# Strassen-type stage of a top-k attention and two-MoE kernel: parity of deferred cosines, earlier due times of joins and snapshots, one pair fewer on shared banks

## The chip, the core and the metric

The kernel runs on one core of one Trainium2 chip. The metric is the device time of one execution in microseconds (us). Three executions of the kernel before took 1436.85, 1238.50 and 1239.03 us, median 1239.03. The profiled execution took 1239.47 us; the profile's own span, from the first to the last instruction, is 1237.7 us, so 1.8 us lie around it.

## What is computed

```python
def _attn_ref(q, k, v):                 # 4 x 8 heads, 576 tokens, head size 64
    scores = scale * np.matmul(q, k.transpose(0, 1, 3, 2))
    kth = np.partition(scores, -top_k, axis=-1)[..., -top_k:-top_k + 1]   # top_k = 32
    scores = np.where(scores >= kth, scores, -1000000000.0)
    attn = np.exp(scores - np.max(scores, axis=-1, keepdims=True))
    attn = attn / (np.sum(attn, axis=-1, keepdims=True) + 1e-09)
    return np.matmul(attn, v)

def _moe_ref(x, w_gate, w_val, w_out):  # 2304 tokens, 512 -> 1536 -> 512
    g = x @ w_gate
    silu = g * (1.0 / (1.0 + np.exp(-g)))
    return silu * (x @ w_val) @ w_out

def _moe2_ref(x, w_in, w_out):          # 2304 tokens, 512 -> 2048 -> 512
    h = x @ w_in
    return (h * np.cos(h)) @ w_out
```

The three run one after the other on the same 2304 tokens; only the last result is an output.

## The kernel before, in words

Attention and the first MoE run interleaved until about 855 us of the span. The change touches what follows: the second MoE.

**Input stage of the second MoE** (`h_proc`, `row_proc`). `h = x @ w_in` is built for blocks of 576 tokens (4 blocks) and, in each block, for 8 pairs of feature tiles of 128 rows, 32 pairs in all. Pair k of the kernel makes the tiles f = 2i (its row 0) and f = 2i + 1 (its row 1), where i = k mod 8. Each pair is a Strassen-Winograd scheme: seven products of six matmuls of 288 columns (line 1401), into three PSUM banks. Between the products stand three snapshots, copies of a bank to SBUF on ScalarE (two of them line 1432, one line 1488), and four joins on VectorE that add a bank and a snapshot into a piece of a row of h (lines 1445, 1466 and 1473) or copy a bank (line 1479). The seventh product, into the first bank, may start only after the join of line 1466 has read that bank; the last join, line 1479, frees it. The products of the next pair may start once the third product of this one is issued.

The scheme's operands are made on the way: weight combinations (adds on VectorE at line 1268, then a rounded part on ScalarE at line 1284 and the remainder on VectorE at line 1287; seven for each two pairs), and combinations of x (line 1351, line 1368 on ScalarE, line 1372 on VectorE; seven for a block). In names such as `w_14_11544` the first number counts these weight tiles: 0 to 6 belong to pairs 0 and 1 of a block, 7 to 13 to pairs 2 and 3, 14 to 20 to pairs 4 and 5, 21 to 27 to pairs 6 and 7.

**Cosines** (`cosine`). h * cos(h) takes three ScalarE operations (lines 1535, 1548, 1551) and two on VectorE (lines 1543, 1552). Half of the feature tiles get it here, 576 tokens wide, before they are stored to the DRAM tensor `gd`. The other half is stored raw, and gets it in the output stage, 512 elements wide. Which half is said by group number: tiles of groups 1 and 3 (`LATE`) are the deferred ones.

**Output stage** (`piece_proc`, `o_proc`, `wout2_proc`). For each of 18 tiles of 128 tokens and each of the four groups, one DMA brings four feature tiles of `gd` (`gr`), the deferred groups get their cosine, the piece is split into a rounded part and a remainder (lines 1643 and 1647), and 12 matmuls of 512 columns (line 1672) add it to the output bank with the weight tiles `W2O` (lines 1589, 1597, 1600).

**What sets the order.** A planner (`Plan`) goes through all work with estimated costs and, whenever an engine is free in its model, emits the ready item with the smallest due number; the order that comes out is fixed for each engine, and engines run it in order and wait on semaphores. The due number of a pair's snapshots and joins is the pair's own time plus an offset minus 30; that of the second MoE's weight combinations is `T2 - 62.0 + 10.0 * q + n`, where the pair's own time is `T2 + 5.6 * k`.

**Banks.** There are eight PSUM banks. The table `banks` gives pair 0 the banks 3, 4, 5. The pairs from `ALONE` up to `BOTH` then take (0, 1, 2) and (3, 4, 5) in turn, and from pair `BOTH` on the pairs go round all eight, three at a time, starting again at bank 0:

```python
    elif k < BOTH:
        banks.append([bank(b) for b in ((0, 1, 2), (3, 4, 5))[(k - ALONE) % 2]])
    else:
        banks.append([bank((turn8 + n) % 8) for n in range(3)])
        turn8 += 3
```

With `BOTH = 6`, pair 5 has banks 0, 1, 2, and so has pair 6.

The functions that the change touches, as they stand before:

Of the kernel before, what the change touches and what calls it, by code (L numbers as in the profile page):

```python
# [29 lines left out]
NF2 = F2 // 128  # L30
# [11 lines left out]
NCB = NTOK // CB  # L42
NLAST = 3
ALONE = 1
BOTH = 6
AHEAD = 4
WLEAD = 20.0
LATE = (1, 3)
# [116 lines left out]
def topk_attention_moe_moe(ctx: ExitStack, tc: tile.TileContext, qT, kT, vP, w1, wo1, w2, out):  # L165
    nc = tc.nc
# [954 lines left out]
    HN = CB // 2  # L1121
# [265 lines left out]
    def h_proc(j, i):  # L1387
        k = j * NPR + i
        q, side = divmod(i, 2)
        due = b_due(k)  # L1390
        ps, rows = {}, {}
        row_ev = [Event(2), Event(2)]
        pb = lambda: pools["pb"]

        def product(n, b, start):
            if start:
                ps[b] = bank_tile(banks[k][b][2])[:, :HN]
            w, x = W2I[q, n].rearrange("p h (v k f) -> p h v k f", v=2, k=2), X2[j, n]
            for kk in range(2):
                for m, (a, e) in enumerate(((0, 0), (0, 1), (1, 0))):  # L1400
                    nc.tensor.matmul(ps[b], w[:, a, side, kk], x[:, e, kk],  # L1401
                                     start=start and kk == 0 and m == 0, stop=kk == 1 and m == 2,
                                     skip_group_check=True)

        def step(n, b, start, offset):
            yield ev_w2[q, n]
            yield ev_x2[j, n]
            if start:
                ring, index, number = banks[k][b]
                if 4 <= number < 6:  # L1410
                    yield ev_ph
                yield ring.gate(index)
            end = yield "PE", 0.8, lambda: product(n, b, start), due + offset, False
            if i == NPR - 1:
                r_xc.free(SEVEN * j + n, end, plan)
            if j == NCB - 1 and side:
                ev_wfree[q, n].set(end, plan)
            return end

        def free(b, t):  # L1420
            ring, index, number = banks[k][b]
            ring.free(index, t, plan)

        snaps = {}

        def snap(name, b, offset):
            ring = (r_s1, r_s2)[name]
            yield ring.gate(k)

            def fn():  # L1430
                snaps[name] = pb().tile([128, HN], F32, tag=f"s{name}", name="s", bufs=ring.n)
                nc.scalar.activation(snaps[name], ps[b], AF.Copy)

            t = yield "ACT", 0.33, fn, due + offset - 30, True
            return t

        def row(r):
            if r not in rows:
                rows[r] = pb().tile([128, CB], F32, tag=f"h{r}", name="h", bufs=(r_ha, r_hb2)[r].n)
            return rows[r]  # L1440

        def c11(e0):
            yield e0
            yield r_ha.gate(k)
            t = yield "DVE", 0.37, lambda: nc.vector.tensor_add(row(0)[:, :HN], ps[1], snaps[0]), due + 3.0 - 30, True
            free(1, t)
            r_s1.free(k, t, plan)
            row_ev[0].set(t, plan)

        if k:  # L1450
            yield ev_mm[k - 1, 2]
        end = yield from step(0, 0, True, 0.0)
        e_s1, e_s2, e_c22, e_p2, e_p3 = Event(), Event(), Event(), Event(2), Event()

        def first():
            t = yield from snap(0, 0, 1.0)
            e_s1.set(t, plan)
            e_p2.set(t, plan)

        def second():  # L1460
            t = yield from snap(1, 0, 3.5)
            e_s2.set(t, plan)

        def c22(start):
            yield r_hb2.gate(k)
            t = yield "DVE", 0.37, lambda: nc.vector.tensor_add(row(1)[:, HN:], ps[0], snaps[2]), due + 6.0 - 30, True  # L1466
            r_s3.free(k, t, plan)
            row_ev[1].set(t, plan)
            e_c22.set(t, plan)

        def c12():
            yield e_s2
            t = yield "DVE", 0.37, lambda: nc.vector.tensor_add(row(0)[:, HN:], ps[2], snaps[1]), due + 8.0 - 30, True
            free(2, t)
            r_s2.free(k, t, plan)
            row_ev[0].set(t, plan)

        def c21():
            t = yield "DVE", 0.36, lambda: nc.vector.tensor_copy(row(1)[:, :HN], ps[0]), due + 8.5 - 30, True
            free(0, t)  # L1480
            row_ev[1].set(t, plan)

        def third():
            yield r_s3.gate(k)

            def fn():
                snaps[2] = pb().tile([128, HN], F32, tag="s3", name="s3", bufs=r_s3.n)
                nc.scalar.activation(snaps[2], ps[2], AF.Copy)

            t = yield "ACT", 0.33, fn, due + 4.0 - 30, True  # L1490
            e_s3.set(t, plan)

        e_s3 = Event()
        plan.start(first(), end + plan.LAT["PE"])
        end = yield from step(1, 1, True, 0.1)
        e_p2.set(end + plan.LAT["PE"], plan)
        ev_mm[k, 1].set(end, plan)
        plan.start(c11(e_p2))
        end = yield from step(2, 2, True, 0.2)
        plan.start(third(), end + plan.LAT["PE"])  # L1500
        ev_mm[k, 2].set(end, plan)
        yield e_s1
        end = yield from step(3, 0, False, 0.3)
        plan.start(second(), end + plan.LAT["PE"])
        yield e_s3
        end = yield from step(4, 2, False, 0.4)
        e_p3.set(end + plan.LAT["PE"], plan)
        yield e_s2
        end = yield from step(5, 0, False, 0.5)
        t = end + plan.LAT["PE"]  # L1510
        plan.start(c22(t), t)
        plan.start(after(e_p3, c12()))
        yield e_c22
        end = yield from step(6, 0, False, 0.6)
        plan.start(c21(), end + plan.LAT["PE"])
        for r in range(2):
            plan.start(row_proc(k, r, rows, row_ev[r]))
# [1 line left out]
    r_s1, r_s2, r_s3 = Ring(2), Ring(1), Ring(1)  # L1519
    ev_wfree = {(q, n): Event() for q in range(NF2 // 4) for n in range(SEVEN)}  # L1520

    early = [n for n in range(NCB * NF2) if n % NF2 // 4 not in LATE]
    turn_of = {n: i for i, n in enumerate(early)}

    def cosine(i, h, width, due):
# [48 lines left out]
    def o_due(n):  # L1574
        return b_due(NCB * NPR) + n * 2.8
# [35 lines left out]
        (t, m) for t in range(AHEAD, NTOK // 128) for m in range(NG)]  # L1611
    place = {x: n for n, x in enumerate(ORDER)}

    def piece_proc(t, m):
        n = place[t, m]
        due = o_due(n) - 6.0
        for j in range(t * 128 // CB, (t * 128 + 127) // CB + 1):
            yield ev_gd[j]
        if n:
            yield ev_gt[n - 1]  # L1620
        yield r_xr.gate(6 * NCB + n)
        st = {}

        def load():
            st["x"] = pools["pb"].tile([128, 2, HN], F32, tag="xr", name="gr", bufs=r_xr.n).rearrange(
                "p a b -> p (a b)")[:, :DM]
            nc.sync.dma_start(st["x"].rearrange("p (f n) -> p f n", f=4),
                              gd[:, 4 * m:4 * m + 4, t * 128:t * 128 + 128])

        end = yield "DMA", 1.2, load, due - 6.0, True  # L1630
        ev_gt[n].set(end - 2.0, plan)
        x = st["x"]
        if m in LATE:
            i = len(early) + len(LATE) * t + LATE.index(m) if t >= AHEAD else len(early) + LATE.index(m) * AHEAD + t
            x, end = yield from cosine(i, st["x"], DM, due)
        if n:
            yield ev_gh2[n - 1]
        yield r_xc.gate(SEVEN * NCB + n)

        def hi():  # L1640
            GP[n] = pools["pb"].tile([128, 2, 2, HN], F32R, tag="xc", name="gp", bufs=r_xc.n).rearrange(
                "p a b c -> p a (b c)")[:, :, :DM]
            nc.scalar.activation(GP[n][:, 0], x, AF.Copy)

        end = yield "ACT", 0.52, hi, due, True
        ev_gh2[n].set(end, plan)
        end = yield "DVE", 0.62, lambda: nc.vector.tensor_sub(GP[n][:, 1], x, GP[n][:, 0]), due, True
        if m in LATE:
            r_r2.free(i, end, plan)
        r_xr.free(6 * NCB + n, end, plan)  # L1650
        ev_gp[n].set(end, plan)

    def o_proc(t):
# [4 lines left out]
        for m in range(NG):  # L1658
            n = place[t, m]
            yield ev_gp[n]  # L1660
            for f in range(4 * m, 4 * m + 4):
                yield ev_w2o[f]
                if f == 0:
                    yield ring.gate(index)

                def part(f=f, n=n):
                    if f == 0:
                        st["o"] = bank_tile(number)
                    g = GP[n]
                    cs = slice(f % 4 * 128, f % 4 * 128 + 128)  # L1670
                    for i, (a, b) in enumerate(((0, 0), (1, 0), (0, 1))):
                        nc.tensor.matmul(st["o"], g[:, a, cs], W2O[f][:, b], start=f == 0 and i == 0,  # L1672
                                         stop=f == NF2 - 1 and i == 2)

                end = yield "PE", 0.7, part, o_due(n) + f % 4 * 0.7, False
            r_xc.free(SEVEN * NCB + n, end, plan)
        yield r_ot.gate(t)

# [93 lines left out]
```

## Time and profile before

| what | value |
|---|---|
| median of three runs | 1239.03 us |
| profiled execution | 1239.47 us |
| its span | 1237.7 us |
| TensorE busy (matmul) | 1179.8 us, 95% |
| VectorE busy | 1003.4 us, 81% |
| ScalarE busy | 936.6 us, 76% |
| GpSimd busy | 575.6 us, 47%, none after 800 us |
| mean granted TensorE clock | 0.993 |
| longest chain of waits | 56% TensorE; lines 1672 (16%), 1401 (13%), 902 (10%) lead it |

A share of busy time is a mean over stages. To read what an edit of the second MoE is worth, look at the stretch from 809 us on, where its first product runs, and there at the times in which TensorE sits idle.

### The profile page before, as it was taken

The numbers are of one execution on the slowest core, as the hardware profiler recorded it, in microseconds if no ns is written. First come the engines' busy times: TensorE is split into PE (matmuls) and PEld (weight loads), VectorE is DVE, ScalarE is ACT, GpSimd is POOL, SyncE is SP. The second block draws the span as 40 slices with busy tenths as digits, with TensorE's granted clock in tenths as the row PEclk, the third lists the DMA queues.
The fourth block names the chain that finished last, engine by engine and source line by source line (L and its number), as shares of the span: only waits on it lengthen the run. The fifth ranks groups of instructions, "written<-read, shape, count | busy, mean of one in ns | idle before, by whom it ended". The sixth has DMA issues, their size and how long they took to land.

```text
span 1237.7 us, 23277 instructions
## 1 busy us (share of the span) xinstructions
PE 1179.8 (95%) x7720; PEld 1021.3 (83%) x7720; DVE 1003.4 (81%) x1984; ACT 936.6 (76%) x2085; POOL 575.6 (47%) x1036
## 2 busy tenths in 40 slices
PE   6699988999999999999999999998999999999998
PEld 3477646898888898888898898988899998888887
DVE  6999999999999999998999996267867778544441
ACT  4789988899889889897898887445757668765651
POOL 4898976777677776776777765300000000000000
PEclk9899989999999999999999999999999999999999
DMA  7555555665555565566555533463344376433430
GB/s 256 165 176 163 178 173 186 205 203 178 185 171 170 189 196 154 169 185 187 188 166 174 162 105 95 154 212 117 134 139 135 130 228 212 144 107 115 124 106 26
DMA packets 138984, 199.95 MB, mean 162 GB/s; under 512 B 19312, under 2 KB 88432, under 8 KB 138864
## 3 DMA queue, kind: packets, MB, share of 16 engines
q1 hardware_dynamic: 138704, 198.40, 50.6%
q8 instruction: 61, 1.00, 0.3%
q14 instruction: 59, 0.48, 0.1%
q10 hardware_dynamic: 160, 0.07, 0.0%
HBM read 152.28 MB, written 46.14 MB: 160 GB/s over the span
## 4 chain that ended last, share of the span: by engine, by line
PE 56%; DMA 7%; ACT 7%; DVE 4%; POOL 4%; issue 2%; SPq 0%; POOLq 0%; ACTq 0%; DVEq 0%
PE b L1672 16%; PE b L1401 13%; PE gv L902 10%; PE y L1066 7%; PE av L747 3%; PE sc L597 2%; PE gvl L902 2%; PE tp L691 2%; DMA kx<-in_kT 2%; DVE m L627 1%; DVE w L630 1%; DMA w2d<-w_raw 1%; DMA wo<-wo 1%; DMA qx<-in_qT 1%; DMA w_raw<-in_w 1%
## 5 line engine op out<-in xcount | busy, mean ns | idle before, releaser
L627 DVE MAX8 m<-w 128x8 f32<-128x576 f32 x432 | 310.9, 747 | 1.8
L902 PE MATMUL gv<-x,w 128*128 128x256 f32 x2016 | 284.0, 288 | 2.2 <-ACT hg L869 2.1
L902 PEld LDWEIGHTS gv<-x,w 128*128 128x128 f32 x2016 | 259.2, 190 | 9.3 <-ACT hg L869 3.5
L630 DVE MATCH_REPLACE8 w<-m,w 128x576 f32<-128x576 f32 x288 | 213.2, 742 | 0.0
L1672 PE MATMUL b<-w2o,gp 128*128 128x512 f32 x864 | 202.1, 395 | 0.0
L1672 PEld LDWEIGHTS b<-w2o,gp 128*128 128x128 f32 x864 | 162.1, 188 | 39.0
L1401 PE MATMUL b<-xc,w 128*128 128x288 f32 x1344 | 184.2, 298 | 6.1 <-DVE h L1466 5.6
L1401 PEld LDWEIGHTS b<-xc,w 128*128 128x128 f32 x1344 | 181.5, 189 | 7.6 <-DVE h L1466 6.3
L1066 PE MATMUL y<-wo,gh 128*128 128x512 f32 x400 | 148.7, 414 | 5.2 <-DMA wo<-wo 2.5
L627 DVE MAX8 m<-s 128x8 f32<-128x576 f32 x144 | 107.6, 747 | 17.6 <-ACT s L602 15.9
L658 ACT ACTIVATE e<-s,b 128x576 f32<-128x576 f32 x144 | 114.2, 794 | 9.2 <-POOL b L641 9.0
L669 ACT ACTIVATE e<-e,b 128x576 f32<-128x576 f32 x144 | 114.2, 793 | 2.8 <-POOL b L645 0.2
L602 ACT ACTIVATE s<-sc 128x576 f32<-128x576 f32 x144 | 95.4, 663 | 21.4 <-PE sc L590 15.8
L630 DVE MATCH_REPLACE8 w<-m,s 128x576 f32<-128x576 f32 x144 | 106.8, 742 | 0.0
L691 PE MATMUL tp<-ident,e 128*128 128x128 f32 x648 | 98.9, 276 | 6.4 <-ACT pt L697 3.1
L697 ACT ACTIVATE pt<-tp 128x512 f32<-128x512 f32 (+1 forms) x216 | 101.5, 501 | 4.3 <-PE tp L691 2.9
L1066 PEld LDWEIGHTS y<-wo,gh 128*128 128x128 f32 x400 | 74.7, 188 | 28.0 <-issue 4.1
L597 PE MATMUL sc<-K,q 128*128 128x288 f32 (+1 forms) x512 | 92.2, 307 | 2.6 <-ACT s L602 2.3
L691 PEld LDWEIGHTS tp<-ident,e 128*128 128x128 f32 x648 | 77.9, 142 | 16.9 <-ACT pt L697 6.7
L1066 PE MATMUL y<-wo,gl 128*128 128x512 f32 x208 | 85.6, 418 | 6.1 <-POOL gl L965 3.0
L965 POOL TENSOR_TENSOR gl<-vv,gh 128x256 fp32r<-128x256 f32 x84 | 62.0, 738 | 42.5 <-ACT gh L961 29.0
L597 PEld LDWEIGHTS sc<-K,q 128*128 128x128 f32 (+1 forms) x512 | 73.4, 184 | 8.3 <-ACT s L602 3.7
(115 smaller groups left out, 2093.7 us busy)
## 6 DMA issues: line engine op xcount, KB each, us to landing
wo<-wo SPq DMA_DIRECT2D x96, 512.0 KB, 3.7
gr<-gd SPq DMA_DIRECT2D x72, 256.0 KB, 3.1
w_raw<-in_w SPq DMA_DIRECT2D x32, 511.8 KB, 4.3
V<-in_vP SPq DMA_DIRECT2D x52, 256.0 KB, 3.0
w<-in_w SPq DMA_DIRECT2D x24, 511.5 KB, 5.6
kx<-in_kT SPq DMA_DIRECT2D x64, 144.0 KB, 3.2
wo<-wo SPq DMA_DIRECT2D x36, 256.0 KB, 3.0
gd<-r SPq DMA_DIRECT2D x32, 288.0 KB, 2.2
```

The lines of the kernel that those rows point to most:

```text
L597: nc.tensor.matmul(sc[:r1, s, :HALF], q[:, a, (t - t0) * 128:(t - t0) * 128 + r1], k[:, s * HALF:s * HALF + HALF], start=a == 0, stop=a == 1)
L602: nc.scalar.activation(st["s"], sc[:, :, :HALF], AF.Copy)
L627: nc.vector.max(out=st["m"][:, 8 * i:8 * i + 8], in_=st["w"] if i else st["s"])
L630: nc.vector.match_replace(out=st["w"], in_to_replace=st["m"][:, 8 * i:8 * i + 8], in_values=st["w"] if i else st["s"], imm_value=LOWEST)
L658: nc.scalar.activation(st["e"], st["s"], AF.Prelu, bias=st["b"][:, 1:2], scale=SCALE, alpha=STEEP)
L669: nc.scalar.activation(st["e"], st["e"], AF.Exp, bias=st["b"][:, 2:3], scale=1.0, accum_out=smT[c, p, g][:, j:j + 1])
L691: nc.tensor.transpose(st["ps"][:, j - j0], e[:, j * 128:j * 128 + 128], ident)
L697: nc.scalar.activation(pt[:, j0:j1], st["ps"][:, :j1 - j0], AF.Copy)
L902: nc.tensor.matmul(gv[g], W1[f, kk // 2][:, a, g, kk % 2], m, start=kk == 0 and i == 0, stop=kk == KT - 1 and i == 2)
L1066: nc.tensor.matmul(bank, m, w, start=f == 0 and n == 0, stop=f == NF1 - 1 and n == len(terms) - 1)
L1401: nc.tensor.matmul(ps[b], w[:, a, side, kk], x[:, e, kk], start=start and kk == 0 and m == 0, stop=kk == 1 and m == 2, skip_group_check=True)
L1672: nc.tensor.matmul(st["o"], g[:, a, cs], W2O[f][:, b], start=f == 0 and i == 0, stop=f == NF2 - 1 and i == 2)
```

## The change

Three things are edited. First, tiles are grouped by parity: group 1 holds the odd tiles among 0 to 7 and group 3 those among 8 to 15, where before groups were four tiles in a row. The deferred tiles are thus row 1 of each pair, where before they were both rows of pairs 2, 3, 6 and 7 of each block. The output stage's DMA, weights and matmuls follow that grouping. Second, in the due numbers of the three snapshots and four joins 30 becomes 90. Third, `BOTH` becomes 5: pair 4 is now the last that takes turns between two sets, pair 5 has banks 0, 1, 2, pair 6 has 3, 4, 5, pair 7 has 6, 7, 0.

```diff
-BOTH = 6
+BOTH = 5
...
-            t = yield "ACT", 0.33, fn, due + offset - 30, True
+            t = yield "ACT", 0.33, fn, due + offset - 90, True
...
-            t = yield "DVE", 0.37, lambda: nc.vector.tensor_add(row(0)[:, :HN], ps[1], snaps[0]), due + 3.0 - 30, True
+            t = yield "DVE", 0.37, lambda: nc.vector.tensor_add(row(0)[:, :HN], ps[1], snaps[0]), due + 3.0 - 90, True
...
-            t = yield "DVE", 0.37, lambda: nc.vector.tensor_add(row(1)[:, HN:], ps[0], snaps[2]), due + 6.0 - 30, True
+            t = yield "DVE", 0.37, lambda: nc.vector.tensor_add(row(1)[:, HN:], ps[0], snaps[2]), due + 6.0 - 90, True
...
-            t = yield "DVE", 0.37, lambda: nc.vector.tensor_add(row(0)[:, HN:], ps[2], snaps[1]), due + 8.0 - 30, True
+            t = yield "DVE", 0.37, lambda: nc.vector.tensor_add(row(0)[:, HN:], ps[2], snaps[1]), due + 8.0 - 90, True
...
-            t = yield "DVE", 0.36, lambda: nc.vector.tensor_copy(row(1)[:, :HN], ps[0]), due + 8.5 - 30, True
+            t = yield "DVE", 0.36, lambda: nc.vector.tensor_copy(row(1)[:, :HN], ps[0]), due + 8.5 - 90, True
...
-            t = yield "ACT", 0.33, fn, due + 4.0 - 30, True
+            t = yield "ACT", 0.33, fn, due + 4.0 - 90, True
...
-    early = [n for n in range(NCB * NF2) if n % NF2 // 4 not in LATE]
+    def group_of(f):
+        return f // 8 * 2 + f % 2
+
+    early = [n for n in range(NCB * NF2) if group_of(n % NF2) not in LATE]
...
+    def members(m):
+        return slice(m // 2 * 8 + m % 2, m // 2 * 8 + 8, 2)
+
...
-                              gd[:, 4 * m:4 * m + 4, t * 128:t * 128 + 128])
+                              gd[:, members(m), t * 128:t * 128 + 128])
...
-            for f in range(4 * m, 4 * m + 4):
+            for v, f in enumerate(range(NF2)[members(m)]):
...
-                    cs = slice(f % 4 * 128, f % 4 * 128 + 128)
+                    cs = slice(v * 128, v * 128 + 128)
```

Where the instructions stand now is shown at three places. In these rows the cosine's lines are 3 higher in the changed kernel than before (1543 is now 1546, 1552 is 1555).

The first is VectorE's order while pair 1 is under way. `L1466 ... s_11521` is pair 1's join before its seventh product. Before:

```order
L1268 TENSOR_TENSOR wr<-wr 128x512
L1287 TENSOR_TENSOR w_19_11566<-wr,w_19_11566 128x512
L1268 TENSOR_TENSOR wr<-wr 128x512
L1287 TENSOR_TENSOR w_16_11589<-wr,w_16_11589 128x512
L1268 TENSOR_TENSOR wr<-wr 128x512
L1287 TENSOR_TENSOR w_17_11603<-wr,w_17_11603 128x512
L1287 TENSOR_TENSOR w_20_11576<-wr,w_20_11576 128x512
L1287 TENSOR_TENSOR w_18_11609<-wr,w_18_11609 128x512
L1466 TENSOR_TENSOR h<-b,s_11521 128x288
L1473 TENSOR_TENSOR h<-b,s 128x288
L1445 TENSOR_TENSOR h<-b,s 128x288
```

Now, where the same join is `s_11518`:

```order
L1268 TENSOR_TENSOR wr<-wr 128x512
L1473 TENSOR_TENSOR h<-b,s 128x288
L1287 TENSOR_TENSOR w_14_11543<-wr,w_14_11543 128x512
L1466 TENSOR_TENSOR h<-b,s_11518 128x288
L1287 TENSOR_TENSOR w_15_11557<-wr,w_15_11557 128x512
L1268 TENSOR_TENSOR wr<-wr 128x512
L1445 TENSOR_TENSOR h<-b,s 128x288
L1268 TENSOR_TENSOR wr<-wr 128x512
L1479 COPY h<-b 128x288
L1287 TENSOR_TENSOR w_16_11594<-wr,w_16_11594 128x512
L1287 TENSOR_TENSOR w_17_11606<-wr,w_17_11606 128x512
```

The join stood behind all seven remainders of the third set of weights (14 to 20); it now stands behind the first of them, and the joins come between the weight rows.

The second place is TensorE's order from the end of pair 4 into pair 6 (weights 14 to 20 are used by pair 4 and again by pair 5, 21 and up by pair 6). Before:

```order
L1401 MATMUL b<-xc,w_17_11603 128x288 x6
L1401 MATMUL b<-xc,w_20_11576 128x288 x6
L1401 MATMUL b<-xc,w_18_11609 128x288 x6
L1401 MATMUL b<-xc,w_19_11566 128x288 x6
L1401 MATMUL b<-xc,w_20_11576 128x288 x6
L1401 MATMUL b<-xc,w_21_11783 128x288 x6
L1401 MATMUL b<-xc,w_22_11793 128x288 x6
```

Now:

```order
L1401 MATMUL b<-xc,w_20_11571 128x288 x6
L1401 MATMUL b<-xc,w_17_11606 128x288 x6
L1401 MATMUL b<-xc,w_18_11645 128x288 x6
L1401 MATMUL b<-xc,w_21_11825 128x288 x6
L1401 MATMUL b<-xc,w_19_11560 128x288 x6
L1401 MATMUL b<-xc,w_22_11835 128x288 x6
L1401 MATMUL b<-xc,w_23_11874 128x288 x6
L1401 MATMUL b<-xc,w_20_11571 128x288 x6
```

Before, no product of pair 6 stood ahead of pair 5's last one (the second `w_20`); now three do, two of them between pair 5's sixth (`w_19`) and its seventh.

The third place is VectorE's order ahead of the first remainder of the next token block (line 1372, used by pair 8). Before:

```order
L1543 SCALAR_TENSOR_TENSOR r<-h,k 128x576
L1466 TENSOR_TENSOR h<-b,s_11863 128x288
L1552 TENSOR_TENSOR r<-r,h 128x576
L1479 COPY h<-b 128x288
L1543 SCALAR_TENSOR_TENSOR r<-h,k 128x576
L1552 TENSOR_TENSOR r<-r,h 128x576
L1543 SCALAR_TENSOR_TENSOR r<-h,k 128x576
L1445 TENSOR_TENSOR h<-b,s 128x288
L1552 TENSOR_TENSOR r<-r,h 128x576 x2
L1372 TENSOR_TENSOR xc<-xr,xc 128x576
```

Now:

```order
L1466 TENSOR_TENSOR h<-b,s_11840 128x288
L1445 TENSOR_TENSOR h<-b,s 128x288
L1268 TENSOR_TENSOR wr<-wr 128x512
L1287 TENSOR_TENSOR w_24_11903<-wr,w_24_11903 128x512
L1479 COPY h<-b 128x288
L1287 TENSOR_TENSOR w_25_11926<-wr,w_25_11926 128x512
L1287 TENSOR_TENSOR w_27_11851<-wr,w_27_11851 128x512
L1546 SCALAR_TENSOR_TENSOR r<-h,k 128x576 x2
L1372 TENSOR_TENSOR xc<-xr,xc 128x576
```

Before, all cosine rows of pairs 4 and 5 stood ahead of it, four pairs of operations; now the cosines of these two pairs are two pairs of operations, their second operations stand behind it, and the last weight remainders stand close in front of it.

## Rows read from the trace of the kernel before

**Rows 1.** Page: engine's busy time; costliest groups (busy, mean ns | idle before, releaser)

```profile
PE 1179.8 (95%) x7720; PEld 1021.3 (83%) x7720; DVE 1003.4 (81%) x1984; ACT 936.6 (76%) x2085; POOL 575.6 (47%) x1036
L1672 PE MATMUL b<-w2o,gp 128*128 128x512 f32 x864 | 202.1, 395 | 0.0
L1401 PE MATMUL b<-xc,w 128*128 128x288 f32 x1344 | 184.2, 298 | 6.1 <-DVE h L1466 5.6
```

**Rows 2.** Windows: length, busy PE, PEld, DVE, ACT, POOL (count), clock, DMA share, GB/s

```profile
857.00:861.00 4.00, 0.80 (x7) 0.46 (x5) 4.00 (x8) 1.86 (x6) 0.00 (x0) 1.00 0.27 77
861.00:864.40 3.40, 3.40 (x15) 3.39 (x15) 1.91 (x5) 2.21 (x5) 0.00 (x0) 0.50 0.33 107
864.40:879.70 15.30, 15.30 (x117) 15.30 (x116) 10.95 (x21) 10.08 (x21) 0.00 (x0) 1.00 0.49 168
879.70:887.00 7.30, 4.39 (x29) 3.69 (x28) 6.48 (x14) 5.46 (x11) 0.00 (x0) 1.00 0.05 16
887.00:1030.00 143.00, 143.00 (x1075) 143.00 (x1074) 106.83 (x198) 97.36 (x190) 0.00 (x0) 1.00 0.47 161
```

**Rows 3.** Timeline, TensorE, 853 to 1031 us: start, length, instruction, [idle before, releaser]

```profile
853.10 4.38 PE L1401 MATMUL b<-xc,w 128*128 128x288 f32 x30
857.35 0.44 PE L1105 MATMUL y<-ident,yo 128*128 128x128 f32 x2
860.99 3.25 PE L1401 MATMUL b<-xc,w 128*128 128x288 f32 x12 [3.20 <-DVE h L1466]
864.03 0.55 PE L1105 MATMUL y<-ident,yo 128*128 128x128 f32 x2
864.32 5.07 PE L1401 MATMUL b<-xc,w 128*128 128x288 f32 x36
869.23 0.38 PE L1105 MATMUL y<-ident,yo 128*128 128x128 f32 x2
869.36 10.63 PE L1401 MATMUL b<-xc,w 128*128 128x288 f32 x78
881.34 2.67 PE L1401 MATMUL b<-xc,w 128*128 128x288 f32 x18 [1.34 <-DVE h L1466]
885.02 1.05 PE L1401 MATMUL b<-xc,w 128*128 128x288 f32 x6 [1.02 <-DVE h L1466]
886.63 144.27 PE L1401 MATMUL b<-xc,w 128*128 128x288 f32 x1080 [0.55 <-DVE h L1479]
```

**Rows 4.** Timeline, VectorE, 854 to 861 us

```profile
854.46 1.29 DVE L1287 TENSOR_TENSOR w<-wr,w 128x512 fp32r<-128x512 f32 x2
...
858.68 1.89 DVE L1287 TENSOR_TENSOR w<-wr,w 128x512 fp32r<-128x512 f32 x3
860.48 0.45 DVE L1466 TENSOR_TENSOR h<-b,s 128x288 f32<-128x288 f32 x1
```

**Rows 5.** Timeline, VectorE, 874 to 892 us

```profile
874.81 1.28 DVE L1287 TENSOR_TENSOR w<-wr,w 128x512 fp32r<-128x512 f32 x2
...
880.83 0.45 DVE L1466 TENSOR_TENSOR h<-b,s 128x288 f32<-128x288 f32 x1
...
883.85 0.75 DVE L1543 SCALAR_TENSOR_TENSOR r<-h,k 128x576 f32<-128x576 f32 x1
884.51 0.45 DVE L1466 TENSOR_TENSOR h<-b,s 128x288 f32<-128x288 f32 x1
...
886.11 0.46 DVE L1479 COPY h<-b 128x288 f32<-128x288 f32 x1 [0.23 <-PE b L1401]
...
891.65 0.76 DVE L1372 TENSOR_TENSOR xc<-xr,xc 128x576 fp32r<-128x576 f32 x1 [0.31 <-ACT xc L1368]
```

**Rows 6.** Groups by form, 809 to 1237 us: busy us, mean ns of one | idle before

```profile
L1552 DVE TENSOR_TENSOR r<-r,h 128x576 f32<-128x576 f32 x32 | 24.2, 755 | 7.7 <-ACT r L1551 7.7
L1551 ACT ACTIVATE r<-r,halfpi 128x576 f32<-128x576 f32 x32 | 24.7, 772 | 0.4
```

**Rows 7.** Timeline, VectorE: the seventh remainder of the output weights

```profile
1009.23 0.69 DVE L1600 TENSOR_TENSOR w2o<-wr,w2o 128x512 fp32r<-128x512 f32 x1 [0.16 <-ACT w2o L1597]
```

More of the change, by code (lines that the diff above doesn't have):

```diff
@@ L1664, in o_proc, with part @@
                     yield ring.gate(index)
-                def part(f=f, n=n):
+                def part(f=f, n=n, v=v):
                     if f == 0:
@@ L1673, in part @@
                                          stop=f == NF2 - 1 and i == 2)
-                end = yield "PE", 0.7, part, o_due(n) + f % 4 * 0.7, False
+                end = yield "PE", 0.7, part, o_due(n) + v * 0.7, False
             r_xc.free(SEVEN * NCB + n, end, plan)
```

## The prediction

> **What bounds the kernel now.** Start with the page: TensorE is busy 95% of the span, the others less, and its two largest groups show the key difference. The output stage's 864 matmuls never sit idle before they start; the 1344 of the input stage's products do, for 6.1 us in all, and the work that ends most of that idle time is VectorE's join of line 1466 [rows 1]. So in the part of the kernel that the change touches TensorE sets the end, and the most that an edit of order can give there is its idle time and what hangs on it. The windows say where that is: from 887 to 1030 us TensorE is busy all the time, 143.00 of 143.00 us with 1075 instructions, so one takes 0.133 us at the full granted clock; from 857 to 861 us it is busy 0.80 of 4 us, from 861 to 864.4 us busy but granted half the clock, and from 879.7 to 887 us busy 4.39 of 7.30 us [rows 2]. The timeline of TensorE then gives each wait with its releaser: 3.20 us at 860.99, 1.34 at 881.34 and 1.02 at 885.02, all for the join of line 1466, and 0.55 at 886.63 for the copy of line 1479; behind it 1080 matmuls run without one [rows 3].
>
> **What this stretch costs in all.** From 857.35 to 886.63 us, 29.28 us, TensorE did 12 + 36 + 78 + 18 + 6 = 150 matmuls of line 1401 and three pairs of transposes [rows 3]. At 0.133 us the matmuls need 19.95 us; a pair of transposes takes 0.13 us (869.23 to 869.36), three 0.39. That is 20.34 us, so 8.94 us were lost. The parts: waits 3.20 + 1.34 + 1.02 + 0.55 = 6.11; the half clock, where 12 matmuls and a pair of transposes took 860.99 to 864.32 = 3.33 us in place of 12 x 0.133 + 0.13 = 1.73, so 1.60; and 1.23 at the edges of the four waits (a matmul counts to its end, 0.298 us [rows 1], and not to the next start, and the first ones after a wait run slowly). Only the longest wait was followed by the lower clock: that is 1.2 GHz against 2.4.
>
> **The due numbers (30 to 90).** The wait of 3.20 us is pair 1's seventh product. The join that it needs reads the product that opens the row at 853.10; six matmuls on, at about 854.1, that was done. The join started at 860.48, 6.4 us later, because VectorE takes its instructions in order and weight adds and remainders stood ahead of it from 854.46 on, one every 0.60 us (three in 858.68 to 860.48) [rows 3, 4]. In the new order one remainder stands ahead of it. It then starts at about 855.1 and ends at 855.6, when TensorE, which now puts two products in between (853.10 + 18 x 0.133 = 855.5), comes to the seventh. The wait goes, and with it the half clock: 3.20 + 1.60, and its share of the edges. The wait of 1.34 us is the same thing in pair 4: the sixth product is the eleventh of the thirteen groups of six in the row at 869.36, so it starts at about 877.4 and ends at 878.4, and the join starts at 880.83, behind a run of weight rows that began at 874.81 [rows 3, 5]. Put ahead, it ends by 879.0, when TensorE is still busy with the row of 78, which runs to 879.99. So 1.34 goes too. Who is queued behind the joins now: the weight remainders, each join ahead of them costing them 0.37 us (884.51 to the next row is one). They have time: the first one of pair 6's set starts at 874.81 and its product at 886.63, over 11 us later [rows 3, 5]. If TensorE gains 8.9 us some 2 us of that are left, which is thin, and a rival below. The snapshots move ahead on ScalarE in the same way; none of the waits in the stretch names them, so I cost that at nothing.
>
> **One pair fewer on shared banks.** The wait of 1.02 us is pair 5's seventh product. Its sixth, the row of 18's last six matmuls, ended at 884.0; the join started at 884.51 behind one cosine row (883.85) [rows 3, 5]. So 0.5 us is queue, the rest the plain time from product to join to product. TensorE had nothing else to do: pair 6 had the same three banks and could not start until the copy at 886.11 had freed the first, which is the last wait, 0.55. In the new order pair 6 has three other banks, and two of its products, 2 x 6 x 0.133 = 1.6 us, stand between pair 5's sixth and seventh, one of them even ahead of the sixth. They cover 1.02, and the copy no longer holds anything up: 1.57 goes. Pair 7 now gets banks 6, 7 and 0. The first two hold the first MoE's last output tiles, whose last transposes run at 869.23 [rows 3], long before.
>
> **The parity.** The count of cosines is the same, 32 rows in the input stage and 36 pieces in the output stage, and so is the number and size of the DMAs; a row of the stored tensor is read in the same pieces of 128 tokens, only from every second tile. What moves is when: each pair has one cosine, where pairs 0, 1, 4 and 5 of a block had two and the others none. Ahead of pair 8 that takes two cosines out of the fullest stretch of VectorE (6.48 busy of 7.30 us [rows 2]) and puts them into pairs 6 and 7. It frees no TensorE time by itself, since no wait is left after 886.63, so I cost it at nothing; it makes room for what the other two edits pull forward. In the output stage the first piece needs weight tile 6 as its fourth, where it needed tile 3. Tile 6 was ready at 1009.23 + 0.69 = 1009.92 [rows 7], the stage would start at about 1030.7 - 8.9 = 1021.8: covered by 12 us. The stores of cosine rows in SP's queue can delay loads behind them by at most one cosine, five operations of 0.7 to 0.8 us or some 3.6 us [rows 6]; nothing in this stretch waits for a load, and I take zero.
>
> **Sum.** 1239.47 - 8.94 = 1230.5 us, if nothing new appears. A few short waits where the margins have become thin should cost some tenths; I predict **1231 us**, 8 below the median of 1239.03 (which is 0.4 under the profiled execution). Its own range is 1229.5 to 1232.5: undisturbed executions differ by 1.0 us (1238.50 to 1239.47).
>
> **A rule that speaks against it.** Pairs 8 to 31 already go round all eight banks, and TensorE there is busy all the time at a granted clock of 1.00 [rows 2]; so I charge nothing for one pair more that does. The Trainium skill, "TensorE: Matmul & The Clock Gate", section "A second HAM failure mode: psum-queue depth-cycling", says that going through PSUM banks in each iteration can leave TensorE short idle times in which the clock falls and rises again. By that rule the sum would lose part of what it gains; the trace does not agree, with no idle time in those 143 us.
>
> **Rivals.** *The next block's operands come late.* Pair 8's first product stands 12 groups of six behind 886.63, that is 9.6 us: 896.2, and 887.3 once 8.9 us are gained. The first remainder of its operands ended at 891.65 + 0.76 = 892.4 [rows 5], so it must come 5.1 us earlier. Out of its way go two cosines (2 x 2 x 0.67 us of VectorE) and two more second halves that now stand behind it (2 x 0.67), 4.0 us; the missing 1.1 must come from VectorE's idle time, which from 861 to 879.7 us is 18.7 - 12.86 = 5.8 us [rows 2]. If that idle time can't be used 1.1 us come back, if ScalarE's half of the chain (which the row at 891.65 waited for) sets the pace up to 5.1: 1231.6 to 1235.6 us. For it: thin margins at both the weights and x. Against it: the work fits by count.
>
> *Slower: every block boundary pays.* Before, pairs 6 and 7 of each block had no cosine, and that is where VectorE made the next block's operands. Two pairs last 84 x 0.133 = 11.2 us; eight joins (3.0) and eleven combinations at 0.67 (7.4) fill 10.4 of it; two cosines add 2.7 and make 13.1. If the work can't start earlier each of the three boundaries waits 1.9 us, 1236.2 in all; if a whole cosine chain of 3.6 us comes in between, with 1.6 for the clock and 0.3 for the edges, 5.5 each, 1247. The result is slower than before from 3.0 us (8.94 / 3) a boundary on. Against it: VectorE is busy 106.83 of 143 us and ScalarE 97.36 [rows 2], so there is room in the earlier pairs, which have one cosine less.
>
> *It does nothing.* If the join's wait were for its product or snapshot and not for its place, moving it would be idle: 1239. The 6.4 us between product and join speak against it.
>
> *The clock.* If it fell once a block, at 1.60 each [rows 2, 3], 6.4 us come back: 1237. The 143 us at 1.00 speak against it.
>
> **Chances.** Forecast 0.70, late operands 0.17, slow boundaries 0.06, no effect 0.04, clock 0.03. The range 1229 to 1236 holds the forecast and most of the late operands, 0.85 less what the sum may be off. About 2% (25 us) is what a measurement of this kernel can tell from no change; every case above lies within it. So within 2% has 0.97; faster needs 25 us where TensorE's idle time in the stage is 6.1, 0.01; slower needs 1264, a boundary loss far past the worst one above, 0.02.
>
> **What would show it.** Right: no idle time of TensorE from 857 to 890 us, the join of pair 1 within 1.5 us of its product, granted clock 1.00 there, pair 6's first product ahead of pair 5's sixth, first output matmul at about 1022 us. Wrong: new waits of TensorE for line 1372 or 1287, or idle time at the boundaries of pairs 16 and 24.

## The result, and the profile after

The changed kernel took 1227.28 us, median of six executions (1224.92 to 1231.11), beside 1238.54 for the kernel before in the same measurement: a ratio of 0.9917, 95% interval 0.9893 to 0.9940. One of the six executions of the kernel before took 1436.85 us; the ratio leaves it out and is formed from the single executions, so it is not the quotient of the two medians. The forecast of 1231 us is 0.9935 of the median it started from, and that ratio lies inside the interval, but the time itself came out below the range of 1229 to 1236. It moved the way that was forecast, by 11.3 us instead of 8. The profiled execution took 1224.92 us, with a span of 1222.8.

First the page of the changed kernel, the lines that answer to [rows 1] (line 1672 is now 1678):

```profile
PE 1174.4 (96%) x7720; PEld 1019.1 (83%) x7720; DVE 1002.2 (82%) x1984; ACT 936.1 (77%) x2085; POOL 575.9 (47%) x1036
L1678 PE MATMUL b<-w2o,gp 128*128 128x512 f32 x864 | 202.1, 396 | 0.0
L1401 PE MATMUL b<-xc,w 128*128 128x288 f32 x1344 | 182.1, 297 | 0.1
```

The idle time before the products of line 1401 has gone from 6.1 us to 0.1; the output stage had none and has none. VectorE and ScalarE do the same work in the same busy time. The timeline of TensorE answers to [rows 3]; it would give the idle time before a row in brackets, as it does there:

```profile
846.79 5.05 PE L1401 MATMUL b<-xc,w 128*128 128x288 f32 x36
...
851.81 4.24 PE L1401 MATMUL b<-xc,w 128*128 128x288 f32 x30
...
856.03 4.24 PE L1401 MATMUL b<-xc,w 128*128 128x288 f32 x30
...
860.25 155.76 PE L1401 MATMUL b<-xc,w 128*128 128x288 f32 x1164
1015.86 0.87 PE L1678 MATMUL b<-w2o,gp 128*128 128x512 f32 x3
```

Left out are three pairs of transposes. No row has an idle time before it: 1164 matmuls run in one piece into the output stage, which begins at 1015.86 and not at the 1022 of the forecast. The windows of this stretch answer to [rows 2] (length, busy PE, PEld, DVE, ACT, POOL, granted clock, DMA share, GB/s):

```profile
855.00:876.00 21.00, 21.00 (x160) 21.00 (x160) 17.40 (x34) 16.03 (x34) 0.00 (x0) 1.00 0.48 157
876.00:881.00 5.00, 5.00 (x40) 5.00 (x38) 5.00 (x10) 4.68 (x10) 0.00 (x0) 1.00 0.10 36
881.00:1015.00 134.00, 133.94 (x1005) 133.71 (x1004) 101.56 (x188) 92.27 (x178) 0.00 (x0) 1.00 0.50 166
```

The granted clock is 1.00 throughout. From 876 to 881 us VectorE has no idle time at all, just ahead of pair 8, but TensorE does not wait for it. VectorE's timeline at pair 1 answers to [rows 4]:

```profile
847.29 0.68 DVE L1287 TENSOR_TENSOR w<-wr,w 128x512 fp32r<-128x512 f32 x1
847.89 0.45 DVE L1466 TENSOR_TENSOR h<-b,s 128x288 f32<-128x288 f32 x1
848.26 0.68 DVE L1287 TENSOR_TENSOR w<-wr,w 128x512 fp32r<-128x512 f32 x1
```

Pair 1's sixth product is the first of the 36 matmuls from 846.79 on, so it ends at about 846.79 + 5 x 0.133 + 0.30 = 847.8; its join starts at 847.89, not 6.4 us later. At the place of [rows 5], ahead of pair 8:

```profile
875.75 1.42 DVE L1546 SCALAR_TENSOR_TENSOR r<-h,k 128x576 f32<-128x576 f32 x2
877.08 0.75 DVE L1372 TENSOR_TENSOR xc<-xr,xc 128x576 fp32r<-128x576 f32 x1
```

The first remainder of the next block ends at 877.8.

**Where the time went.** Cut each profile at two marks: the start of the first product (line 1401) and the start of the last output matmul (1672, or 1678). What lies between is called the stage below. In the row of a line its last pair of times is the first and the last start. The kernel before, then the changed one, first profiles:

```profile
L1401 PE MATMUL b<-xc,w x1344: 289/297/609, 809.1 to 1035.0; 128*128 128x288 f32 x192
L1672 PE MATMUL b<-w2o,gp x864: 387/396/403, 1030.7 to 1233.7; 128*128 128x512 f32 x173
```

```profile
L1401 PE MATMUL b<-xc,w x1344: 292/297/404, 803.0 to 1020.1; 128*128 128x288 f32 x192
L1678 PE MATMUL b<-w2o,gp x864: 392/396/401, 1015.9 to 1218.8; 128*128 128x512 f32 x173
```

The stage took 1218.8 - 803.0 = 415.8 us in the changed kernel and 1233.7 - 809.1 = 424.6 before. So 8.8 of the 14.9 us between the two spans came from the stage, and 6.1 from the time before its first product, up to which TensorE, VectorE, ScalarE and GpSimd do the same in the same order in both kernels. The first question for the experiments is thus what these 6.1 us are; the second, which edit is worth what.

### The profile page after: what moved, and what is told of

The parts are those of the page before. It is cut to its first block, busy times and chain, and to the rows that moved or that the text cites. A ratio compares the mean times of both kernels' runs of the same rounds, so it can differ in the third digit from the quotient of the medians.

```text
span 1222.8 us, 23301 instructions
## 1 busy us (share of the span) xinstructions
PE 1174.4 (96%) x7720; PEld 1019.1 (83%) x7720; DVE 1002.2 (82%) x1984; ACT 936.1 (77%) x2085; POOL 575.9 (47%) x1036
## 4 chain that ended last, share of the span: by engine, by line
PE 58%; DVE 7%; DMA 6%; ACT 5%; POOL 3%; issue 2%; SPq 0%; POOLq 0%; ACTq 0%; DVEq 0%
PE b L1678 16%; PE b L1401 13%; PE gv L902 10%; PE y L1066 7%; DVE m L627 3%; DVE w L630 3%; PE av L747 2%; PE gvl L902 2%; PE sc L597 2%; PE tp L691 2%; DMA wo<-wo 2%; DMA kx<-in_kT 1%; DMA w2d<-w_raw 1%; DMA w_raw<-in_w 1%; DMA qx<-in_qT 1%
```

## The experiments

**Both kernels once more.** No edit.

> The kernel before, once more, to see how its two halves vary: the time to the first product of line 1401 (809.1 us in the first profile) and the stage from there to the start of the last output matmul of line 1672 (424.6 us). Theory 1 (the change gains only in the stage, and the time to the first product varies by several us from one execution to the next, whatever the kernel): stage 424.6 within 0.5; time to the first product anywhere from 802 to 811 us. Theory 2 (the changed kernel also gets to the first product some 6 us sooner): stage 424.6, and the time to the first product stays at 809 within 1 us, in every execution of this kernel.

> The changed kernel, once more. Theory 1: the stage takes 415.8 us within 0.5 (8.8 less than before), the time to the first product is not tied to 803.0 and lies anywhere from 802 to 811 us; over many runs the two kernels differ by 8.9 us (1239.47 - 8.94 in the prediction), the ratio is near 0.9928. Theory 2: the time to the first product is again 803 within 1 us, and the kernels differ by some 15 us, ratio 0.988.

The kernel before, second profile: the two marks, and TensorE's waits.

```profile
L1401 PE MATMUL b<-xc,w x1344: 292/297/609, 802.0 to 1028.6; 128*128 128x288 f32 x192
L1672 PE MATMUL b<-w2o,gp x864: 387/396/403, 1024.4 to 1227.3; 128*128 128x512 f32 x173
```

```profile
853.60 3.25 PE L1401 MATMUL b<-xc,w 128*128 128x288 f32 x12 [3.21 <-DVE h L1466]
874.95 2.66 PE L1401 MATMUL b<-xc,w 128*128 128x288 f32 x18 [1.34 <-DVE h L1466]
878.63 1.07 PE L1401 MATMUL b<-xc,w 128*128 128x288 f32 x6 [1.02 <-DVE h L1466]
880.25 144.26 PE L1401 MATMUL b<-xc,w 128*128 128x288 f32 x1080 [0.55 <-DVE h L1479]
```

The changed kernel, second profile:

```profile
L1401 PE MATMUL b<-xc,w x1344: 293/297/402, 807.7 to 1024.8; 128*128 128x288 f32 x192
L1678 PE MATMUL b<-w2o,gp x864: 392/396/403, 1020.5 to 1223.5; 128*128 128x512 f32 x173
```

The roles have changed places: the kernel before reaches its first product at 802.0, the changed one at 807.7. The changed kernel's stage is the same as the first time, 415.8 us. That of the kernel before took 425.3 us, 0.7 more than the first time and a little outside what was expected, although the four waits repeat to 0.01 us. What differs is the stretch at the lower clock, which here is longer than the one from 861 to 864.4 us of [rows 2] (columns of the window as above):

```profile
852.00:860.00 8.00, 6.40 (x29) 6.38 (x30) 5.69 (x11) 4.21 (x10) 0.00 (x0) 0.57 0.43 137
```

Twelve executions of this copy of the kernel before went from 1232.65 to 1240.98 us (1236.80 median; ratio to the kernel before 1.0016, 1.0000 to 1.0031). The changed kernel had a median of 1226.84, ratio 0.9934 (0.9915 to 0.9953); the 27 executions of the kernel before beside which both ratios are taken had a median of 1235.45. Theory 1 holds but for those 0.2 us: the gain is the stage's, 8.8 to 9.5 us, and the time before it varies by 7 us whatever the kernel. Theory 2 falls.

**Each edit alone, and each pair.** Six kernels, every one the kernel before with some of the three edits. The diffs are parts of the one shown above:

```diff
e_due, e_par_due, e_due_both:   30 -> 90 in the due numbers of snapshots and joins
e_both, e_par_both, e_due_both: BOTH = 6 -> BOTH = 5
e_par, e_par_due, e_par_both:   group_of, members and the slices that use them
```

> The kernel before with the due numbers alone (30 to 90). As the prediction has it, the waits of 3.20 us (with the lower clock behind it, 1.60) and of 1.34 us go, with their edges some 6.7 us, and the two waits at pair 5 and 6 stay (1.57): stage 424.6 - 6.7 = 417.9. Rival: with TensorE sooner at pairs 4 and 5, whose two cosines a pair are still there, the joins there are waited for again and less is gained: stage 419 to 421.

> The kernel before with BOTH = 5 alone. As the prediction has it, only the waits of 1.02 and 0.55 us go, with their edges some 2.2 us; the waits of 3.20 and 1.34 stay, and the lower clock after the first: stage 424.6 - 2.2 = 422.4. Rival: pair 5's join waits as long, only later, since VectorE is the one that is late there: stage 424.6.

> The kernel before with the grouping by parity alone. The prediction charged it nothing: the joins still stand behind the weight rows and pairs 5 and 6 share banks, so stage 424 to 425.5 us, as before (424.6 and 425.3 in two profiles), and waits of some 3 us for pair 1's join and 1 to 3 us for pair 4's. Rival: the cosines spread evenly leave VectorE free earlier, and half of the waits go: stage 420 to 422.

> Parity and due numbers, BOTH = 6 still. If the three edits simply add, the stage is the changed kernel's plus what BOTH alone gave (0.8 to 1.5 us): 416.6 to 417.3. If the shared banks are the only thing left, TensorE waits at pairs 5 and 6 as it does with the due numbers alone (1.12 and 1.10 us), with edges 2.5 to 3 us: 418.5 to 419.

> Parity and BOTH = 5, the due numbers still minus 30. By the theory that the joins' place in VectorE's order is the main thing, the waits at pair 1 (3 us, with the lower clock behind it) and pair 4 stay: stage 422 to 424. Rival: with even cosines and separate banks the joins are not late any more: 416 to 418.

> Due numbers and BOTH = 5, grouping as before. The prediction put all of the gain on these two edits and nothing on the parity: stage 415.8 to 416.3, as the changed kernel. Rival: the parity is needed to make room on VectorE before pair 8, where the due numbers alone still left a wait of 0.50 us at 891 us; with nothing else to hold TensorE back that wait grows to 1.5 to 2.5 us: stage 417.5 to 418.5.

The stage is taken from one profile each, between the marks; repeated profiles of one kernel gave 424.6 and 425.3, and 415.8 twice. The ratio to the kernel before (95% interval) is from 6 to 12 executions of each kernel, beside 27 of the kernel before (median 1235.45 us) for its own copy, the changed kernel's, due 90 and BOTH 5 alone, and beside 29 (1235.09) for the other four; the 0.9917 is that of the result. The column "low" counts the stretches of the stage in which the granted clock was at the lower level; the prediction priced one at 1.60 us.

| parity | due 90 | BOTH 5 | first product at, us | stage, us | low | median, us | ratio |
|---|---|---|---|---|---|---|---|
| | | | 809.1; 802.0 | 424.6; 425.3 | 1; 1, longer | 1238.54; 1236.80 | 1; 1.0016 |
| x | | | 806.9 | 426.8 | 2 | 1235.34 | 1.0014 (0.9998 to 1.0030) |
| | | x | 807.3 | 423.8 | 1 | 1233.16 | 0.9981 (0.9968 to 0.9994) |
| x | | x | 803.3 | 421.7 | 0 | 1233.31 | 0.9984 (0.9969 to 0.9999) |
| | x | | 807.7 | 419.5 | 0 | 1232.96 | 0.9974 (0.9960 to 0.9989) |
| x | x | | 803.0 | 419.9 | 1 | 1229.75 | 0.9961 (0.9946 to 0.9975) |
| | x | x | 803.7 | 417.7 | 0 | 1227.15 | 0.9944 (0.9926 to 0.9962) |
| x | x | x | 803.0; 807.7 | 415.8; 415.8 | 0; 0 | 1227.28; 1226.84 | 0.9917; 0.9934 |

TensorE's waits of 0.5 us and more after 840 us say why. Due numbers alone:

```profile
877.05 1.07 PE L1401 MATMUL b<-xc,w 128*128 128x288 f32 x6 [1.12 <-DVE h L1466]
879.23 11.53 PE L1401 MATMUL b<-xc,w 128*128 128x288 f32 x84 [1.10 <-DVE h L1479]
891.26 133.13 PE L1401 MATMUL b<-xc,w 128*128 128x288 f32 x996 [0.50 <-DVE h L1466]
```

The waits at pairs 1 and 4 are gone, as forecast. Those at the shared banks are not, and the second doubled (0.55 to 1.10); the stage got 5.1 us shorter, not 6.7: the rival of that run. `BOTH = 5` alone:

```profile
859.27 2.08 PE L1401 MATMUL b<-xc,w 128*128 128x288 f32 x12 [3.21 <-DVE h L1466]
879.66 148.61 PE L1401 MATMUL b<-xc,w 128*128 128x288 f32 x1104 [1.34 <-DVE h L1466]
```

Just the two waits at the shared banks, 1.57 us, are gone; the stage is 0.8 to 1.5 us shorter, between the 2.2 of the theory and the nothing of its rival. The parity alone:

```profile
858.09 3.08 PE L1401 MATMUL b<-xc,w 128*128 128x288 f32 x12 [2.57 <-DVE h L1466]
879.92 2.65 PE L1401 MATMUL b<-xc,w 128*128 128x288 f32 x18 [2.79 <-DVE h L1466]
883.18 1.05 PE L1401 MATMUL b<-xc,w 128*128 128x288 f32 x6 [0.61 <-DVE h L1466]
885.14 145.79 PE L1401 MATMUL b<-xc,w 128*128 128x288 f32 x1080 [0.90 <-DVE h L1479]
```

It mends nothing: the wait at pair 1 is a little shorter, the one at pair 4 doubles (1.34 to 2.79), and the stage is 1.5 to 2.2 us longer, more than either theory gave. Most of that is the clock: behind the last two waits this profile has a second stretch at the lower level, which the kernel before has in neither profile:

```profile
882.00:890.00 8.00, 6.49 (x36) 6.03 (x35) 4.04 (x8) 4.20 (x7) 0.00 (x0) 0.79 0.29 111
```

Less 1.60 for it the stage would be 425.2, within the theory's 424 to 425.5, and the twelve executions can't be told from the kernel before (1.0014). That the parity alone does harm is thus not shown. On top of the other two edits it takes off 1.9 us of the stage (417.7 to 415.8), with no such stretch in any of these profiles; the medians, 1227.15 without it beside 1227.28 and 1226.84 with it, do not show it. The kernel with these two and without it comes out in the rival's range of 417.5 to 418.5 and has one wait left, at 885.47, of 1.29 us where the rival had 1.5 to 2.5. TensorE first, then VectorE ahead of that wait:

```profile
885.47 133.07 PE L1401 MATMUL b<-xc,w 128*128 128x288 f32 x996 [1.29 <-DVE h L1466]
```

```profile
883.26 0.75 DVE L1552 TENSOR_TENSOR r<-r,h 128x576 f32<-128x576 f32 x1
883.93 0.45 DVE L1473 TENSOR_TENSOR h<-b,s 128x288 f32<-128x288 f32 x1
884.30 0.75 DVE L1543 SCALAR_TENSOR_TENSOR r<-h,k 128x576 f32<-128x576 f32 x1
884.96 0.45 DVE L1466 TENSOR_TENSOR h<-b,s 128x288 f32<-128x288 f32 x1
```

VectorE goes from the cosines of pairs 4 and 5 to joins and back without a break, and the joins come late by the cosine rows in between, although the due numbers put them first: the order is fixed on the planner's clock. From 876.4 us on seven cosine rows stand ahead of this join; in the changed kernel, from 875.7 us on, five stand ahead of the like one at 882.44, and the wait is gone. Of the pairs, the two without the shared-bank edit or without the due numbers keep the matching waits:

```profile
872.26 1.06 PE L1401 MATMUL b<-xc,w 128*128 128x288 f32 x6 [1.16 <-DVE h L1466]
874.43 145.65 PE L1401 MATMUL b<-xc,w 128*128 128x288 f32 x1080 [1.11 <-DVE h L1479]
```

(parity and due numbers; 419.9 us, more than either theory gave, with one stretch at the lower clock, told of below), and parity with `BOTH = 5` (421.7, just under its theory):

```profile
854.38 1.87 PE L1401 MATMUL b<-xc,w 128*128 128x288 f32 x12 [2.57 <-DVE h L1466]
874.69 147.47 PE L1401 MATMUL b<-xc,w 128*128 128x288 f32 x1104 [2.73 <-DVE h L1466]
```

Three single edits give -5.1, -0.8 and +2.2 against the first profile of before, together -3.7; the three together give -8.8. At 1.60 us for each stretch at the lower clock, my estimate of what the edits give without it is -3.5, -0.8 and +0.6, together -3.7 again, beside -7.2. They don't add. One reason stands in the rows: where TensorE was mended at pairs 1 and 4 it waited longer at the shared banks (1.12 and 1.10 us for 1.02 and 0.55). In the order due numbers, banks, parity the stage lost 5.1, 1.8 and 1.9 us.

**Which of the seven due numbers.** One execution each, the stage from its profile.

```diff
e_joins: -90 for the four joins on VectorE, snapshots stay at -30
e_snap:  -90 for the snapshots on ScalarE, joins stay at -30
e_join:  -90 for the join of line 1466 alone
```

> The kernel before, with minus 90 for the four joins on VectorE alone; the snapshots on ScalarE keep minus 30. The theory is that VectorE's order is what the due numbers mend, and that ScalarE's costs nothing: stage 419.5 as with both (within 0.5), no wait of 3 us at pair 1. Rival: with the joins early the snapshots become what is late, a wait for lines 1432 or 1488 of 1 us or more appears, and the stage is 421 to 423.

> The kernel before, with minus 90 for the snapshots on ScalarE alone; the joins keep minus 30. Theory: nothing changes, the waits of 3.2 us at pair 1 and 1.34 us at pair 4 for line 1466 stay, stage 424.6 to 425.3. Rival: a snapshot was what the joins waited for: stage 420 to 422.

> The kernel before, with minus 90 for the join of line 1466 alone, the one TensorE is seen waiting for. If that join alone matters, the waits of 3.20 and 1.34 us go and the stage is 419.5 to 420.5. Rival: the joins of lines 1445 and 1473, then still behind the weight rows, hold the next pair's banks and snapshots, and new waits take half of it back: stage 421.5 to 423.5.

The snapshots alone give nothing, 424.6 us, with the same four waits as before (3.21, 1.30, 1.02, 0.55). The joins alone give 422.1, the one join alone 423.2. Both numbers lie in the ranges of the rivals and outside those of the theories, but both profiles have a lower clock that the full set of due numbers has not, so the numbers alone decide nothing. The four joins without the snapshots:

```profile
871.36 1.85 PE L1401 MATMUL b<-xc,w 128*128 128x288 f32 x12 [0.29 <-ACT s L1488]
874.59 1.07 PE L1401 MATMUL b<-xc,w 128*128 128x288 f32 x6 [1.38 <-DVE h L1466]
876.76 15.11 PE L1401 MATMUL b<-xc,w 128*128 128x288 f32 x97 [1.10 <-DVE h L1479]
892.55 131.56 PE L1401 MATMUL b<-xc,w 128*128 128x288 f32 x983 [0.68 <-DVE xc L1372]
```

The waits at pairs 1 and 4 are gone, as the theory had it, but one for a snapshot and one for a remainder of the next block appear. The one for the snapshot is 0.29 us, not the 1 us or more of the rival. From 877 to 881 us the granted clock was 0.57; less 1.60 for that, the stage would be 420.5, beside 419.5 with the snapshots moved too, and two profiles of one kernel have differed by 0.7. The one join alone, and its window at the lower clock:

```profile
855.76 1.86 PE L1401 MATMUL b<-xc,w 128*128 128x288 f32 x12 [0.36 <-ACT s L1488]
858.18 1.87 PE L1401 MATMUL b<-xc,w 128*128 128x288 f32 x12 [0.55 <-DVE h L1479]
877.36 1.06 PE L1401 MATMUL b<-xc,w 128*128 128x288 f32 x6 [1.35 <-DVE h L1466]
880.02 146.95 PE L1401 MATMUL b<-xc,w 128*128 128x288 f32 x1080 [1.60 <-DVE h L1479]
```

```profile
878.00:886.00 8.00, 6.40 (x30) 6.17 (x29) 5.18 (x10) 3.95 (x8) 0.00 (x0) 0.57 0.09 33
```

The wait of 3.2 us is traded for 0.36 and 0.55 at once, and at the shared banks 1.02 and 0.55 become 1.35 and 1.60. So moving one join hands part of the wait on. The waits themselves, added up, do not hang on the clock: 6.1 us before and with the snapshots alone, 3.86 with the one join, 3.45 with the four joins, 2.72 with joins and snapshots. The one join is thus most of it. What the other joins and the snapshots add lowers the wait further but is small, from one profile each, and not settled: by stage the snapshots' share would be some 1 us by the estimate above, hardly more than two profiles of one kernel differ by.

## Why the prediction was right in its sum and wrong in its time

- **What bounds the stage**: right. TensorE's idle time and what hung on it was all there was to gain, and it was gained: after 840 us no wait of TensorE is left in the changed kernel.
- **The sum, 8.94 us**: right as a whole. The stage lost 8.8 us in the first profiles, 9.5 against the second profile of before; the ratio of 0.9935 that it stands for lies in the intervals of both 0.9917 and 0.9934. Its split was not right: 5.1 + 1.8 + 1.9 in the order above, where it had 6.7, 2.2 and nothing.
- **The time, 1231, and its own range of 1229.5 to 1232.5**: wrong, and here is the step that failed. "Undisturbed executions differ by 1.0 us (1238.50 to 1239.47)" was read from three executions, and the sum was taken from the profiled one as if its time were the kernel's. In thirteen profiles of kernels that are alike up to the first product, that product starts anywhere from 802.0 to 809.1 us, 805.3 on average (the ten in the table above, and 804.8, 803.3 and 806.6 in the last three runs). The profile that the sum started from has the latest of all, 3.8 us over that average. 1230.5 less 3.8 is 1226.7, beside 1227.28 and 1226.84 measured. The executions say the same: 27 and 29 later ones of the kernel before had medians of 1235.45 and 1235.09, some 4 us below the 1239.47 of the sum, and 8.94 off these is 1226.5 and 1226.2. Twelve executions of the kernel before spread over 8.3 us, not 1.0; a range of that width about 1231 would just have held the result. That the changed kernel was compared with six executions of the kernel before at or above 1236.68 makes the 11.3 us larger than the stage's gain; whether these were late by chance is not known.
- **Due numbers**: right on the two waits and the clock; too large alone by 0.9 to 1.6 us. The waits left were 1.12, 1.10 and 0.50 us, 2.72 in all, where 1.02 and 0.55 were forecast to stay.
- **Shared banks**: both waits went, alone and in company, as forecast; alone the stage got 0.8 to 1.5 us shorter and not 2.2, and why was not looked into.
- **Parity, costed at nothing by itself**: alone that is nearly so, since most of its +1.5 to 2.2 us is a stretch at the lower clock; beside the other two it took 1.9 us off the stage. The text said that it makes room for what the others pull forward; that was its worth, and it should have had a term, since without it 1.29 us of waiting come back.
- **Rivals**: *late operands* did not come about in the changed kernel, but its mechanism is real: with only the joins moved, TensorE waited 0.68 us for line 1372. *Slow block boundaries*: no wait of TensorE behind 860.25. *No effect* falls. *The clock*: it stayed at 1.00 with one pair more on eight banks. By the rule in the Trainium skill, "TensorE: Matmul & The Clock Gate", section "A second HAM failure mode: psum-queue depth-cycling", part of the gain would have been lost; the trace does not agree.

## What to carry to other kernels

When one engine is the bound and another drains it, put the short draining steps of a chain ahead of bulk preparation on the queue that makes the bound engine wait, and then look again: moving one step handed part of the wait on to others of the chain, and the least wait was left where all of them had moved. Edits of this kind need not add; test them in pairs before calling one useless, since the one that mended nothing alone was worth 1.9 us of the stage in company. Look at the granted clock of each profile before comparing two stages. And forecast the difference from the stage that is touched, but the time from several executions: here a single profile's untouched part was 3.8 us off its average, beside a gain of 8.9.

## What was not expected of the hardware

**The time before the stage varies.** With the same instructions in the same order it ends between 802.0 and 809.1 us. Comparing the two profiles of the kernel before matmul by matmul, the lag of the first grows from 0.5 us at 120 us to 7.2 at 426 and stays between 6 and 8 up to the first product; what sets it off was not tried and stays open.

**The lower clock is not tied to the length of a wait.** The prediction charged it to the wait of 3.20 us and noted that the shorter ones had none. Parity with `BOTH = 5` had waits of 2.57 and 2.73 us; its windows behind them (columns as before):

```profile
857.00:860.00 3.00, 3.00 (x25) 3.00 (x24) 2.07 (x4) 1.52 (x4) 0.00 (x0) 1.00 0.65 221
874.00:877.00 3.00, 2.31 (x17) 2.31 (x18) 2.41 (x6) 1.40 (x3) 0.00 (x0) 1.00 0.03 8
```

The clock stayed at 1.00 (2.4 GHz). Parity with the due numbers had waits of only 1.16 and 1.11 us, 2 us apart, and behind them:

```profile
874.00:877.50 3.50, 3.06 (x13) 3.07 (x14) 2.32 (x5) 1.67 (x3) 0.00 (x0) 0.52 0.22 84
```

There it was 0.52 on average, nearly all at the lower level of 1.2 GHz. Yet the due numbers alone had two waits of the same size as near to each other (1.12 and 1.10 us), and there the clock was 1.00 from 850 to 900 us. And the same four waits in the two profiles of the kernel before had a stretch of different length behind the first. The prediction's charge of 1.60 us was right for the profile it was read from, but what decides whether a wait is followed by such a stretch, and how long it lasts, stays open. In the table, a stage with one and a stage without differ by some 1.6 us for that alone.
